# A new written order for a fused attention and two-MLP kernel, with the turns of the two array halves planned in it

## Chip, cores and metric

One core of one Trainium2 chip. The metric is the device time of one execution in microseconds (us); the kernel before takes 1275.89 us (median of 3 runs, 1275.63 to 1276.41). The work is done by TensorE (PE, with its weight loads shown apart as PEld), VectorE (DVE), ScalarE (ACT), GpSimd (POOL), and SyncE (SP), which starts the transfers.

## What is computed

The reference, cut to what matters. First a softmax-weighted sum over 7 neighbouring positions, per head; then two MLPs, the second with a rational function in the middle:

```python
w = exp(weight_gen - max); w = w / (sum(w) + 1e-9)          # [2, 4096, 8 heads, 7]
out[b, s, h, g] = sum_k w[b, s, h, k] * x_pad[b, s + k, h, g] # 8 heads x 24 = 192 columns
x = out.reshape(8192, 192)
h = x @ moe_w_in;  g = h * sigmoid(h);  x = g @ moe_w_out     # 192 -> 2048 -> 192
h = x @ moe2_w_in
P = a0 + a1*h + a2*h^2 + a3*h^3
Q = 1 + |b0|*|h| + |b1|*h^2
return (P / (Q + 1e-6)) @ moe2_w_out
```

## The kernel before

**Tiles.** The 8192 tokens are done in 16 batches of 512. In each batch both MLPs run over 8 units of 256 of the 2048 middle columns. Values are split in a high and a low part (`xh` and `xl`, `g1h` and `g1l`, `g2h` and `g2l`), and each product is the sum of three or so partial products. Weights are split alike (`wa`, `wb` for the first product of an MLP, `wo` for the second).

**The two halves of the array.** Nearly every matmul uses 64 of the 128 rows of TensorE's array: 9728 matmuls of 64 rows by 512 columns, half of them on the upper 64 rows (half 0), half on the lower (half 1). A matmul of half 0 and one of half 1 run side by side. A *turn* below is the time in which a half does one such matmul. A transpose of 64 columns counts as a quarter of a turn, as in the code (L808, L1015).

**Steps.** A step of TensorE is a small list of matmuls for each half. Its name gives the kind, the unit and the batch, so `K3.9` is step K of unit 3 in batch 9:

- `A`, `K` (first MLP) and `B`, `Q` (second): the first product of a unit, into a PSUM tile `h` of two banks. In `A` half 0 writes bank 0 and half 1 writes bank 1; in `K` it is the other way round.
- `C`, `E`, `I`, `F` (first MLP) and `D`, `P`, `J`, `R` (second): the second product, added into the tile `acc` of the batch. `C`, `I`, `D`, `J` need the high part, the others the low part; again each half writes one bank in two of them and the other bank in the other two.
- `T`, `TR` and `FT`, `FR`: transposes of the attention's result and of the batch's output, in the same two sides.

**A flip.** The two halves never write the same bank at once. Where a step changes which half writes which bank of a tile (K after A, Q after B, a change of side in an `acc`), `Lanes.take` puts a no-operation of SyncE between (L388): it waits for the last matmul of the old side in both halves, and the first matmul of the new side in each half waits for it. Such a change is called a flip here. Matmuls of other tiles may stand between the two sides and keep the array at work meanwhile.

**The other engines.** First MLP: ACT does `S` (silu) and `H` (high part), DVE `L` (low part). Second MLP: ACT `U`, `V`, `N`, `G`, DVE `u`, `w`, `Y`, `g`; then `h` (high part, L451, L453 or L455 on ACT, POOL or DVE) and `l` (low part, L987 on DVE or POOL). Attention products and sums (`M`, `m`, `p`, `r`, `a`) go to DVE or POOL. SP issues all transfers and also holds the flips' waits, in its own order.

**What sets the order.** The string `ORDER` is a list of 3956 steps, written out. Each entry may name an engine (`@1`), a buffer (`:c`), or a table load (`^`). `Plan.run` walks it. A step of TensorE is handed to `Lanes.add`, which puts its matmuls into the queues of the two halves; `Lanes.take` then writes them out one at a time into TensorE's single instruction stream. Which half comes next is decided by two clocks: that half whose clock is behind. A `|` before an entry pushes a clock on, so that one half falls behind the other on purpose:

```python
self.now = max(self.now, self.clock[r])
self.clock[r] = self.now + turns
```

Of the kernel before, what the change touches and what calls it, by code (L numbers as in the profile page):

```python
# [25 lines left out]
D = 192  # L26
# [23 lines left out]
    q0O341 A6.0:A s3m r3.1@1 q1B0a1 E5.0 C1.0 C3.0 a0.1@1:a r2.1@1 H4.0:v q0O3h a1.1 q1O0l0:q L4.0:p q1B0a0 K6.0  # L50
    q1O1l1:c q0O3x |F5.0 S6.0 a3.1@1 |||E4.0 q1B040:B H6.0:n F0.0 q1B041 F3.0 q1A0a0 q1O1l0:o a2.1@1 L6.0:m A7.0:D
    q1O0l1:s q1B0h0 m1.2:b q1A1l0:h F4.0 AW.3 I5.0 q1A040:A q1B0h1 K7.0 q1B0x0 M0.2:t C0.0 q1A0a1 q1B0x1 E6.0 M3.2:w
    S7.0 C6.0 q1A041 q1A0h@1 |T.1:B H7.0:i C4.0 m0.2:l TR.1 q1O0a0 s3d@1 C5.0 C7.0 XH0.1:p L7.0:j q1A1l1:a q1O2l1:e
    q1O2l0:x q1O0a1 q1O040:D |||||E7.0 q1A0x M1.2:q ||I4.0 F6.0 q1O041 I7.0 XL0.1:y q1O0h m2.2:v F7.0 q1O1a1 I6.0
    q1O0x q1O1a0 q1O140:A q1O141 ||||A2.1:D ||K2.1 M2.2:r m3.2@1:k q1A1a0 q1O1h p3.2@1 q1A1a1 EC.0@1:n q1A140:B
    q1O1x EM.0 S2.1 p2.2@1 X.3 q1A141 q1O3l0:c H2.1:s p0.2 q1O3l1:o q1A1h L2.1:v r0.2@1 A1.1:A K1.1 q1O2a0 p1.2@1 cr
    A0.1:D EA.0 S1.1 q1A1x XH1.0:h a0.2:n K0.1 r3.2@1 H1.1:m XL1.0:i A3.1:B S0.1 L1.1:t B0.0:C r1.2@1 a1.2 H0.1:k
    a3.2 q1O240:A K3.1 q1O2a1 r2.2@1 L0.1:l Q0.0 S3.1 m2.3:a q1O241 B5.0:D V0.0:x q1O2h@1 a2.2 H3.1:w m0.3:j q1O2x
    Q5.0 U0.0:r L3.1:b B3.0:A M0.3:u V5.0:g u0.0 F0.1:B Q3.0 p0.3@1 U5.0:q w0.0 F2.1 V3.0:e F1.1 I0.1 Y5.0 I1.1
    q1O3a0 F3.1 U3.0:j u5.0 B2.0:C u3.0 C1.1 ^^N5.0 E1.1 Y0.0 w3.0 Q2.0 G5.0 w5.0 E0.1 E3.1 q1O3a1 E2.1 U2.0:m  # L60
    B1.0:A N0.0 C2.1 q1O340:D q1O341 C0.1 g5.0 q1O3h Q1.0 V2.0:k q1O3x I2.1 h5.0:v u2.0 M2.3:g |A5.1:D V1.0:s U1.0:l
    w2.0 K5.1 r0.3@1 G0.0 u1.0 l5.0@1:b A4.1:C w1.0 C3.1 ^S5.1 K4.1 p2.3 g0.0 h0.0@2:t A7.1:A H5.1:c S4.1 I3.1
    l0.0@1:x H4.1:q K7.1 L5.1:f C5.1 S7.1 L4.1:o |A6.1:D H7.1:a Y1.0 r2.3@1 E4.1 K6.1 F4.1 S6.1 L7.1:p B4.0:C M3.3:y
    H6.1:r B6.0:A m3.3:o L6.1:w C6.1 E5.1 ^^N1.0 Y2.0 E7.1 Q4.0 G1.0 Y3.0 R0.0:D I6.1 F5.1 N2.0 g1.0 G2.0 R5.0
    h1.0@2:s D0.0 N3.0 g2.0 I5.1 s3e P0.0 l1.0:f F7.1 h2.0@1:k P5.0 M1.3@1:p Q6.0 U4.0:b l2.0@1:l s3t R1.0 G3.0 J1.0
    C4.1 V6.0:x E6.1 g3.0 s3n@1 D5.0 U6.0:r D1.0 F6.1 h3.0@1:c u6.0 I4.1 J0.0 Y6.0 V4.0:w s3s C7.1 l3.0@1:t P2.0
# [28 lines left out]
    N6.2 J1.2 FE.1@1 R5.2 M2.6:m A0.4:B G6.2 FA.1 EA.3 O.1 A1.4:A g6.2 XH1.3:a D3.2 G7.2 XL1.3:i h6.2:w P5.2 K0.4
    g7.2 B0.3:C ^S0.4 l6.2:r D6.2 H0.4:x m2.6@1:j Q0.3 h7.2@1:b L0.4:t p2.6@1 P6.2 K1.4 U0.3:d l7.2:j A2.4:B V0.3:l
    D4.2 M3.6:s S1.4 u0.3 |K2.4 H1.4:f s4d@1 w0.3 J4.2 S2.4 R7.2 L1.4:c R2.2 r0.6@1 H2.4:y B2.3:C Y0.3 B1.3:A L2.4:g
    ^^N0.3 Q2.3 M1.6@1:e E1.4:B V2.3:u R6.2 p3.6 C0.4 U2.3:k E0.4 Y2.3 Q1.3 G0.3 u2.3 w2.3 F1.4 I0.4 U1.3:v m1.6:c
# [179 lines left out]
class Plan:  # L278
# [25 lines left out]
    def run(self, engines, preload, lanes):  # L304
# [19 lines left out]
        for entry in ORDER.split():  # L324
            head, _, slot = entry.partition(":")
# [16 lines left out]
            else:  # L342
# [781 lines left out]
```

## Time and profile before

| | us |
|---|---|
| median of 3 runs | 1275.89 |
| the profiled execution, its own time | 1275.2 |
| span in its trace | 1273.4 |
| outside the span (launch and end) | 1.8 |
| PE busy | 1223.8 (96%) |
| DVE busy | 1096.0 (86%) |
| ACT busy | 1047.5 (82%) |
| POOL busy | 470.0 (37%) |

PE's busy time counts a matmul from its start to its modelled end, and two run side by side, so 96% busy is not 96% of what the array can do: the distance between the starts of two matmuls of the same half tells more. The granted clock of TensorE is at its full level (2.4 GHz) nearly all the time, with mean 0.991 over the span.

### The profile page before, as it was taken

Reading aid. Unit: us, or ns where it says so; the run is one execution under the profiler, and the core shown is the slowest. Engines: PE = TensorE matmul, PEld = TensorE weight load, DVE = VectorE, ACT = ScalarE, POOL = GpSimd, SP = SyncE. Lnnn points to the kernel's source line nnn. Section 1 sums busy time; section 2 is a strip of 40 time slices with the busy share of each in tenths; the row PEclk is TensorE's granted clock in tenths of the full one; section 3 lists DMA queues with packets and bytes.
Section 4 is the critical chain, followed back from the end, with each engine's and each line's share of the span. In section 5 each row is a group of like instructions: output and inputs, shape, how many; then the busy total and the mean of one; then the engine's idle time right before and its main releaser. Section 6 shows DMA issues by size and latency. Waiting matters only on the chain.

```text
span 1273.4 us, 24930 instructions
## 1 busy us (share of the span) xinstructions
PE 1223.8 (96%) x10332; PEld 1013.4 (80%) x10332; DVE 1096.0 (86%) x1037; ACT 1047.5 (82%) x1023; POOL 470.0 (37%) x311
## 2 busy tenths in 40 slices
PE   4889999999999999999999999999999999999997
PEld 4667777999888777789888787787777888898776
DVE  7889978999888879788989888878787989988897
ACT  3769788888988877698988788878888798899985
POOL 5565554344443422324232531440521513322322
PEclk8989999999999999999999999999999999999999
DMA  7650101010101010101002010010000001000000
GB/s 208 194 171 1 62 1 47 10 44 28 43 26 39 14 40 1 31 10 32 22 5 68 1 56 1 21 40 1 22 32 1 22 13 45 1 22 2 10 14 25
DMA packets 17753, 45.42 MB, mean 36 GB/s; under 512 B 2412, under 2 KB 9194, under 8 KB 17640
## 3 DMA queue, kind: packets, MB, share of 16 engines
q1 hardware_dynamic: 17640, 43.83, 11.2%
q8 instruction: 81, 1.33, 0.4%
q14 instruction: 32, 0.26, 0.1%
HBM read 31.73 MB, written 7.90 MB: 31 GB/s over the span
## 4 chain that ended last, share of the span: by engine, by line
PE 75%; ACT 8%; DVE 6%; issue 2%; SPq 1%; DMA 0%; POOL 0%; DVEq 0%; ACTq 0%
PE acc L795 38%; PE h L795 35%; DVE t L960 1%; ACT t L947 1%; ACT y L971 1%; ACT y L951 1%; DVE t L957 1%; ACT y L974 1%; PE to L1015 1%; PE tp L808 1%; ACT h L902 1%; ACT g1h L906 1%; DVE g1l L910 1%; SPq L928 1%; DVE t L977 1%
## 5 line engine op out<-in xcount | busy, mean ns | idle before, releaser
L795 PE MATMUL h<-xh,wa 64*128 64x512 f32 x2048 | 508.6, 401 | 13.2 <-DVE t L960 2.9
L795 PEld LDWEIGHTS h<-xh,wa 64*128 64x128 f32 x2048 | 303.1, 185 | 79.3 <-SPq L388 39.6
L795 PE MATMUL h<-xl,wa 64*128 64x512 f32 x1024 | 337.7, 390 | 0.1
L795 PE MATMUL h<-xh,wb 64*128 64x512 f32 x1024 | 336.2, 390 | 0.0
L795 PE MATMUL acc<-g1h,wo 64*128 64x512 f32 x1536 | 329.8, 397 | 4.9 <-DVE wo L623 1.8
L795 PE MATMUL acc<-g2h,wo 64*128 64x512 f32 x1536 | 311.3, 393 | 2.4 <-SPq L388 0.6
L795 PEld LDWEIGHTS acc<-g1h,wo 64*128 64x128 f32 x1536 | 224.3, 185 | 36.7 <-SPq L388 13.5
L987 POOL TENSOR_TENSOR g2l<-t,g2h 128x1024 fp32r<-128x1024 f32 x65 | 170.5, 2626 | 212.0 <-DVE g2h L455 98.0
L795 PEld LDWEIGHTS acc<-g2h,wo 64*128 64x128 f32 x1536 | 216.9, 184 | 31.0 <-SPq L388 11.4
L795 PE MATMUL acc<-g1l,wo 64*128 64x512 f32 x1024 | 239.9, 397 | 1.6 <-DVE g1l L910 0.7
L795 PE MATMUL acc<-g2l,wo 64*128 64x512 f32 x1024 | 236.4, 394 | 1.0 <-DVE t L960 0.3
L910 DVE TENSOR_TENSOR g1l<-h,g1h 128x1024 fp32r<-128x1024 f32 x128 | 155.6, 1220 | 62.6 <-ACT g1h L906 50.7
L957 DVE TENSOR_TENSOR t<-t,h 128x1024 f32<-128x1024 f32 x128 | 155.6, 1216 | 37.8 <-ACT y L951 19.9
L902 ACT ACTIVATE h<-h 128x1024 f32<-128x1024 f32 x128 | 129.3, 1011 | 70.8 <-PE h L795 65.2
L795 PEld LDWEIGHTS h<-xl,wa 64*128 64x128 f32 x1024 | 173.6, 185 | 14.7 <-DVE xl L829 0.8
L795 PEld LDWEIGHTS h<-xh,wb 64*128 64x128 f32 x1024 | 172.8, 185 | 14.1
L966 DVE SCALAR_TENSOR_TENSOR y<-y,b_sb 128x1024 f32<-128x1024 f32 x128 | 168.8, 1325 | 11.0 <-ACT y L951 10.8
L977 DVE SCALAR_TENSOR_TENSOR t<-t,a_sb,y 128x1024 f32<-128x1024 f32 x128 | 166.7, 1312 | 12.8 <-ACT y L974 11.5
L947 ACT ACTIVATE t<-h,a_sb 128x1024 f32<-128x1024 f32 x128 | 153.6, 1202 | 24.7 <-PE h L795 23.0
L795 PE MATMUL h<-xl,wb 64*128 64x512 f32 x512 | 169.3, 389 | 0.0
L960 DVE SCALAR_TENSOR_TENSOR t<-t,a_sb,h 128x1024 f32<-128x1024 f32 x128 | 163.5, 1279 | 6.5 <-ACT y L951 3.3
L728 POOL TENSOR_TENSOR pr<-xw,aw 128x768 f32<-128x768 f32 (+1 forms) x74 | 109.6, 1491 | 158.0 <-PE acc L795 82.0
(81 smaller groups left out, 1847.7 us busy)
## 6 DMA issues: line engine op xcount, KB each, us to landing
xw<-in_x_dram SPq DMA_DIRECT2D x14, 960.0 KB, 4.9
raw<-in_moe_w_out_dram SPq DMA_DIRECT2D x16, 383.5 KB, 5.1
out_dram<-of SPq DMA_DIRECT2D x15, 384.0 KB, 2.3
e<-e SPq DMA_DIRECT2D x32, 128.0 KB, 2.3
raw<-in_moe_w_in_dram SPq DMA_DIRECT2D x16, 255.9 KB, 6.6
raw<-in_moe_w_in_dram SPq DMA_DIRECT2D x4, 511.8 KB, 4.7
aw<-wsm SPq DMA_DIRECT2D x14, 112.0 KB, 2.4
sm<-in_weight_gen_dram SPq DMA_DIRECT2D x3, 448.0 KB, 3.4
```

The costliest lines, as they stand in the source:

```text
L728: e.tensor_tensor(out=p.rearrange("p k (h g) -> p k h g", g=G), in0=st[xw][:, j + k0:j + k0 + n, :].rearrange("p k (h g) -> p k h g", g=G) ...
L795: return pe.matmul(out=out, lhsT=w, rhs=x, start=start, stop=stop)
L808: return lambda: pe.transpose(out=st[tp][:, a, j * P + r * DL:j * P + (r + 1) * DL], in_=columns(a, j, r), identity=ident[HALF[r], HALF[r]],)
L902: act.activation(out=st[hb], in_=st[hb], func=AF.Silu)
L906: act.activation(out=t, in_=st[hb], func=AF.Copy)
L910: dve.tensor_tensor(out=t, in0=st[hb], in1=st[gh].bitcast(F32), op=ALU.subtract)
L947: act.activation(out=q, in_=st[hb], func=AF.Identity, scale=a_sb[:, 3:4], bias=a_sb[:, 2:3])
L957: dve.tensor_tensor(out=st[t], in0=st[t], in1=flat(), op=ALU.mult)
L960: dve.scalar_tensor_tensor(out=st[t], in0=st[t], scalar=a_sb[:, 1:2], in1=flat(), op0=ALU.add, op1=ALU.mult)
L966: dve.scalar_tensor_tensor(out=st[y], in0=st[y], scalar=b_sb[:, 0:1], in1=st[y], op0=ALU.add, op1=ALU.mult)
L977: dve.scalar_tensor_tensor(out=st[t], in0=st[t], scalar=a_sb[:, 0:1], in1=st[y], op0=ALU.add, op1=ALU.mult)
L987: e.tensor_tensor(out=q, in0=st[t], in1=st[gh].bitcast(F32), op=ALU.subtract)
```

## The change

Three things change together.

1. `ORDER` is another list of the same 3956 steps: other places, other buffers, and for some steps another engine.
2. The `|` marks are gone. 784 entries carry `>n` or `<n` instead: in this step half 1 stands n turns behind (`>`) or ahead of (`<`) half 0. An entry without a mark has both halves level.
3. `Lanes.add` gives each matmul a planned time when its step is added, and the writing-out goes by these times, rather than by clocks that move as matmuls are written out. `take` and `drain` only compare the times at the heads of the two queues. Flips are made as before.

```diff
+import re
 ORDER = """
-    r1.1@1 |||E3.0 H5.0:g q0O2x A4.0:B q1A0l1:u X.2 q0O3a0 p3.1@1 L5.0:k E1.0 K4.0 q0O3a1 q0O340:D r0.1@1 F1.0 S4.0
+    A6.0:A C3.0 K6.0<2 E3.0<2 p3.1@1 M1.1@1:w A7.0:D<1 H4.0:h S6.0 H6.0:j C4.0<1 L4.0:i q1O1l0:g K7.0<3 L6.0:q
...
-            name = entry.strip("^|").partition(":")[0].partition("@")[0]
+            name = re.split("[:@<>]", entry.lstrip("^"))[0]
...
+            entry, way, lag = re.match("([^<>]*)([<>]?)(.*)", entry).groups()
+            lag = int(lag or 0) * (-1 if way == "<" else 1)
...
-                    lanes.add(name, fn(engines[engine]), bars)
+                    lanes.add(name, fn(engines[engine]), lag)
...
-    def add(self, name, group, bars):
+    def add(self, name, group, lag):
         tile_key, side, turns, rows = group
+        self.clock[1] = max(self.clock[1], self.clock[0] + lag)
+        self.clock[0] = max(self.clock[0], self.clock[1] - lag)
         for r in range(2):
             for emit in rows[r]:
-                self.queue[r].append((name, tile_key, side, turns, emit))
+                self.queue[r].append((self.clock[r], name, tile_key, side, emit))
+                self.clock[r] += turns
         self.left[name] = sum(map(len, rows))
-        if bars:
-            r = self.clock[1] < self.clock[0]
-            self.clock[r] = min(self.clock[r] + bars, self.clock[1 - r])
         while all(self.queue):
-            self.take(self.clock[1] < self.clock[0])
+            self.take(self.queue[1][0][0] < self.queue[0][0][0])
...
-        self.now = max(self.now, self.clock[r])
-        self.clock[r] = self.now + turns
...
-            r = int(self.clock[1] < self.clock[0])
-            self.take(r if self.queue[r] else 1 - r)
+            self.take(bool(self.queue[1]) and (not self.queue[0] or self.queue[1][0][0] < self.queue[0][0][0]))
```

Two places on TensorE show what moves. A row is an instruction; `x2` is two alike in a row; a row that waits for `SP_sequencer` is the first matmul behind a flip.

**Unit 3 of batch 9, first MLP (A3.9, then K3.9).** Rows of `h` belong to A3.9 or K3.9, rows of `acc_7869` to step R of the batch at work in the second MLP. Before:

```order
L795 MATMUL h<-xh_8071,wb_75 128x512
L795 MATMUL acc_7869<-g2l,wo_78 128x512 [waits SP_sequencer_49]
L795 MATMUL h<-xl_8090,wa_71 128x512
L795 MATMUL acc_7869<-g2l,wo_78 128x512
L795 MATMUL h<-xl_8090,wb_75 128x512
L795 MATMUL h<-xh_8071,wa_71 128x512 [waits SP_sequencer_49]
L795 MATMUL acc_7869<-g2l,wo_78 128x512
L795 MATMUL h<-xh_8071,wa_72 128x512
```

and in the change:

```order
L809 MATMUL h<-xl_8097,wa_71 128x512 x2
L809 MATMUL h<-xl_8097,wb_75 128x512 x2
L809 MATMUL acc_7855<-g2h,wo_78 128x512 [waits Pool_49]
L809 MATMUL acc_7855<-g2h,wo_78 128x512 x4
L809 MATMUL h<-xh_8067,wa_71 128x512 [waits SP_sequencer_49]
L809 MATMUL acc_7855<-g2h,wo_78 128x512
L809 MATMUL h<-xh_8067,wa_72 128x512
```

Before, the last matmul of A3.9 stands right ahead of the first of K3.9. Now five matmuls of the second MLP's `acc` stand between them.

**Unit 1 of batch 6, first MLP (A1.6, then K1.6).** Before:

```order
L795 MATMUL h<-xl_5234,wa_71 128x512
L795 MATMUL h<-xl_5234,wb_75 128x512
L795 MATMUL h<-xh_5188,wa_71 128x512 [waits SP_sequencer_49]
L795 MATMUL h<-xh_5188,wa_72 128x512
L795 MATMUL acc_5252<-g2l,wo_78 128x512
```

and in the change:

```order
L809 MATMUL h<-xl_5159,wb_75 128x512 x2
L809 MATMUL h<-xh_5157,wa_71 128x512 [waits DVE_49]
...
L809 MATMUL h<-xh_5157,wa_72 128x512 x2
L809 MATMUL h<-xh_5157,wb_75 128x512 x2
L809 MATMUL h<-xl_5159,wa_71 128x512 x2
L809 MATMUL h<-xl_5159,wb_75 128x512 x2
L809 MATMUL h<-xh_5157,wa_71 128x512 [waits SP_sequencer_49]
```

Before, the last two matmuls of A1.6, both of half 1, are followed at once by K1.6. Now the whole of A0.6, the unit next to it, stands between.

## Rows read from the trace of the kernel before

**Rows 1.** The page: engines, and the chain that ended last by engine.

```profile
span 1273.4 us, 24930 instructions
...
PE 1223.8 (96%) x10332; PEld 1013.4 (80%) x10332; DVE 1096.0 (86%) x1037; ACT 1047.5 (82%) x1023; POOL 470.0 (37%) x311
...
PE 75%; ACT 8%; DVE 6%; issue 2%; SPq 1%; DMA 0%; POOL 0%; DVEq 0%; ACTq 0%
```

**Rows 2.** Windows of 50 us: their bounds, length, each engine's busy time, clock, DMA.

```profile
0.00:50.00 50.00, 30.66 (x207) 25.75 (x207) 41.57 (x55) 26.65 (x35) 25.25 (x28) 0.86 0.80 221
50.00:100.00 50.00, 45.11 (x317) 33.60 (x318) 40.07 (x52) 32.48 (x41) 34.09 (x29) 0.93 0.43 144
250.00:300.00 50.00, 50.00 (x439) 47.30 (x437) 48.99 (x47) 45.12 (x43) 22.40 (x14) 1.00 0.10 30
450.00:500.00 50.00, 47.89 (x382) 37.99 (x380) 41.27 (x37) 41.76 (x40) 10.37 (x5) 1.00 0.06 21
```

**Rows 3.** PE in order of time round the flip of K3.9: start, length, operation.

```profile
709.01 0.39 PE L795 MATMUL h<-xl,wa 64*128 64x512 f32 x1
...
709.23 0.39 PE L795 MATMUL h<-xl,wb 64*128 64x512 f32 x1
709.71 0.50 PE L795 MATMUL h<-xh,wa 64*128 64x512 f32 x1
...
710.05 0.39 PE L795 MATMUL h<-xh,wa 64*128 64x512 f32 x1
```

**Rows 4.** PE in order of time round the flip of Q3.5, batch 5.

```profile
491.26 0.39 PE L795 MATMUL h<-xl,wb 64*128 64x512 f32 x1
491.29 0.61 PE L795 MATMUL acc<-g1h,wo 64*128 64x512 f32 x3
491.78 0.49 PE L795 MATMUL h<-xh,wa 64*128 64x512 f32 x1
...
492.11 0.39 PE L795 MATMUL h<-xh,wa 64*128 64x512 f32 x2
```

**Rows 5.** PE in order of time round the flip of F3.7, batch 7.

```profile
574.21 0.39 PE L795 MATMUL h<-xl,wa 64*128 64x512 f32 x1
...
574.43 0.39 PE L795 MATMUL acc<-g1l,wo 64*128 64x512 f32 x1
...
574.66 0.53 PE L795 MATMUL acc<-g1l,wo 64*128 64x512 f32 x2
```

**Rows 6.** Weight loads that wait for SP: us in total, times, longest.

```profile
PEld h L795 <- SPq L388: 39.6, 86, 1.6
PEld acc L795 <- SPq L388: 32.6, 73, 1.4
```

**Rows 7.** Groups of instructions that change their engine or count.

```profile
L987 POOL TENSOR_TENSOR g2l<-t,g2h 128x1024 fp32r<-128x1024 f32 x65 | 170.5, 2626 | 212.0 <-DVE g2h L455 98.0 <-ACT g2h L451 56.7 <-DVE t L977 16.4
...
L987 DVE TENSOR_TENSOR g2l<-t,g2h 128x1024 fp32r<-128x1024 f32 x63 | 76.8, 1231 | 4.3 <-PE acc L795 2.0 <-POOL g2h L453 1.4 <-PE h L795 0.3
...
L451 ACT ACTIVATE g2h<-t 128x1024 fp32r<-128x1024 f32 x54 | 56.6, 1056 | 9.2 <-DVE t L977 4.8 <-PE acc L795 2.4 <-DVE ao L748 1.2
...
L453 POOL TENSOR_SCALAR g2h<-t 128x1024 fp32r<-128x1024 f32 x45 | 54.5, 1216 | 295.7 <-DVE t L977 114.1 <-DVE t L957 61.4 <-PE h L795 49.2
```

**Rows 8.** DVE's longest wait: us in total, times, longest.

```profile
DVE g1l L910 <- ACT g1h L906: 50.7, 48, 4.2
```

**Rows 9.** Matmuls that wait for SP: us in total, times, longest.

```profile
PE h L795 <- SPq L388: 2.4, 3, 1.2
PE acc L795 <- SPq L388: 2.3, 7, 0.9
```

**Rows 10.** Step Y on DVE: shortest, median and longest of 128.

```profile
L966 DVE SCALAR_TENSOR_TENSOR y<-y,b_sb x128: 1270/1277/2572, 105.5 to 1255.9; 128x1024 f32<-128x1024 f32 x128
```

**Rows 11.** One slow Y on DVE, and POOL at that time.

```profile
986.45 2.37 DVE L966 SCALAR_TENSOR_TENSOR y<-y,b_sb 128x1024 f32<-128x1024 f32 x1
...
985.32 5.77 POOL L987 TENSOR_TENSOR g2l<-t,g2h 128x1024 fp32r<-128x1024 f32 x2 [10.08 <-PE acc L795]
```

More of the change, by code (lines that the diff above doesn't have):

```diff
@@ L50 @@
[L50 to L54, printed above, removed]
@@ L95 @@
[L95 to L98, printed above, removed]
-    J7.2 V1.3:x F0.4 r3.6@1 X.7 B3.3:C N2.3 u1.3 p1.6@1 D7.2 s4e w1.3 P7.2 G2.3 Q3.3 r2.6@1 A3.4:A U3.3:j C2.4 Y1.3
@@ new lines @@
+    w6.10 V4.10:x U4.10:q A6.11:C h1.10:l l1.10:e F4.11 B7.10:B E5.11 u4.10 w4.10 Q7.10 l0.10@1:c p0.13 F5.11
+    V7.10:m h3.10:d l3.10@1:y I5.11 K6.11>2 M1.13:v A7.11:D>2 C5.11>2 U7.10:o u7.10 w7.10 S6.11 H6.11:s K7.11
+    r0.13@1 L6.11:k I6.11 J0.10:B>2 R1.10>4 S7.11 H7.11:h ^^N5.10 L7.11:p R0.10>4 Y6.10 C6.11>4 E6.11>2 N6.10 G6.10
+    P2.10>2 Y7.10 Y4.10 P3.10>2 N4.10 G4.10 P1.10>2 E7.11>2 P0.10>2 T.12:C>2 D3.10>2 F6.11 D2.10 g6.10 TR.12<2
+    I7.11<2 FT.9:D R3.10 R2.10 F7.11 J2.10 C7.11>2 FR.9 D0.10 g4.10 XH0.12:y G5.10 XL0.12:s A1.12:C<2 EC.11@1:i
@@ new lines @@
+    C1.12:C>4 C0.12>2 V1.11:n U1.11:w u0.11 w0.11 Y1.11 A3.12:A G3.11 F0.12 P6.10 D6.10 Y0.11 K3.12<2 E2.12<2
+    R6.10<2 N1.11 u1.11 w1.11 G1.11 E1.12<2 B5.11:D<2 I1.12<2 Q5.11 g1.11 g3.11 Y2.11 E0.12 N0.11 ^S3.12 H3.12:b
+    D5.10 L3.12:n U5.11:o V5.11:a m3.13:q h3.11:x I2.12<2 F3.12 I0.12 u5.11 w5.11 A4.12:A>2 ^^N2.11 G2.11 FC.10:i
+    p3.13 r3.13 E3.12>2 C3.12>2 A5.12:D g2.11 K4.12 K5.12 F2.12 B6.11:B I3.12 G0.11 ^S5.12 H5.12:n S4.12 H4.12:m
+    F1.12>2 Q6.11>2 g0.11 Y5.11 a3.13@1 m2.13:b L5.12:q C2.12>2 A7.12:D I4.12 U6.11:p V6.11:l L4.12:d K7.12>2
@@ new lines @@
+    A6.12:A>2 E4.12>2 C4.12>2 K6.12 h2.11@1:j S7.12 H7.12:f u6.11 w6.11 M2.13:e S6.12 p2.13@1 h0.11:c l0.11@1:k
+    H6.12:m C5.12 C7.12<2 Y6.11 r2.13 ^^N6.11 G6.11 B4.11:B<4 L7.12:y F4.12<4 I5.12<4 J2.11:D<2 F7.12 Q4.11 l2.11:b
+    L6.12:s P0.11 F6.12 a2.13@1 l3.11:n R0.11 T.13:A I6.12 g6.11 h1.11@2:e l1.11:v V4.11:t N5.11 Y4.11 TR.13>2
+    D3.11>2 G5.11 U4.11:k E7.12 P2.11 g5.11 P1.11 E6.12 P3.11 XH0.13:w XL0.13:d u4.11 E5.12 C6.12 J0.11<2 F5.12
+    I7.12 h6.11:m N4.11 h5.11@1:l G4.11 w4.11 l6.11@1:h g4.11 h4.11@2:q FT.10:A>2 D0.11>2 FR.10 D6.11 D1.11<2
@@ new lines @@
+    p2.14@1 K1.13<2 S1.13 R7.11<2 J6.11<2 FC.11:q H1.13:h L3.13:p M3.14@1:m L1.13:x A2.13:A B3.12:B m0.14@1:i Y0.12
+    FT.11:D K2.13 S2.13 FR.11 FE.11 FA.11 C0.13:C Q3.12<2 H2.13:k p0.14 L2.13:n I1.13<2 A5.13:D U3.12:s E0.13
+    r0.14@1 a0.14:e E3.13 r2.14@1 O.11 B1.12:A V3.12:i ^^N0.12 G0.12 I0.13 F3.13>2 Q1.12>2 V1.12:y C1.13>2 u3.12
+    w3.12 E2.13 E1.13 p3.14 Y3.12 B5.12:B Y1.12 I3.13 F0.13>2 U1.12:p u1.12 w1.12 Q5.12>2 N3.12 G3.12 U5.12:h
+    C3.13>2 g0.12 h2.12@2:q A4.13:A V5.12:f u5.12 w5.12 C2.13 r3.14 K4.13<2 ^S4.13 H4.13:o F2.13<2 a2.14@1 g3.12
@@ new lines @@
+    I3.14<2 L4.14:u M1.15:d g0.13 p1.15@1 Q5.13 E3.14 m2.15:x E2.14 A7.14:A A5.14:B U5.13:v V5.13:n F2.14 K5.14
+    S5.14 K7.14 I4.14 S7.14 H5.14:i u5.13 w5.13 Y5.13 r3.15 p2.15 H7.14:l r2.15@1 a2.15 h2.13:x L5.14:p A6.14:D>2
+    L7.14:w C4.14>2 K6.14 F4.14 FT.12:B F5.14 S6.14 H6.14:y FR.12 B7.13:A L6.14:g FE.12@1 FA.12 h1.13:e r1.15@1
+    a1.15 E4.14 E5.14 Q7.13 ^^G4.13 a3.15@1 g4.13 V7.13:s U7.13:m B6.13:D J2.13:B C6.14>2 E6.14 Q6.13 E7.14 C5.14
+    Y7.13 N5.13 G5.13 N3.13 u7.13 h4.13:d l4.13@1:u N7.13 V6.13:p J1.13<2 w7.13 T.15:A F7.14 F6.14 D4.13 G7.13
@@ new lines @@
+    h3.14@2:f A4.15:A>2 C0.15>2 K4.15 Q4.14 C1.15 L5.15:c A7.15:B<2 l3.14:t I5.15<2 S4.15 H4.15:x V4.14:e K7.15
+    g1.14 L4.15:i U4.14:b F5.15 A6.15:A S7.15 H7.15:q u4.14 E5.15 w4.14 K6.15 E4.15 E3.15 h1.14@1:p S6.15 E2.15
+    C4.15 C7.15<2 B6.14:C<4 h0.14:c l0.14@1:j I1.15<4 F4.15<2 I7.15<2 L7.15:g Y4.14 ^^N5.14 G5.14 H6.15:o I6.15
+    g5.14 Q6.14>2 C6.15>2 L6.15:r E6.15 C5.15 E7.15<2 P2.14:B<2 h5.14:w N4.14 G4.14 V6.14:h F7.15<1 F6.15 I4.15
+    g4.14 B7.14:A>2 Y6.14 U6.14:m u6.14 w6.14 FT.13:C>2 N6.14 EC.15:y h4.14@1:g l5.14:u D2.14>2 EM.15 FR.13 FE.13
@@ L267 @@
+    D3.15 P3.15<2 l6.15:b P5.15 g4.15 Y7.15 u7.15 h4.15@1:f l4.15@1:s N7.15 G7.15 w7.15 g7.15 h7.15@2:w l7.15:p
+    D6.15 P6.15<1 R6.15 J5.15 FT.14:C>2 R5.15>2 J4.15>2 J6.15>4 R4.15 O.13 D4.15 P4.15<2 D7.15<1 P7.15 FR.14 R7.15
+    J7.15 FE.14@1 FA.14 O.14 FC.15:v FT.15:D FR.15 FE0.15 FA0.15 FE1.15@1 O0.15 FA1.15 O1.15
 """
@@ L324, in run @@
         for entry in ORDER.split():
+            entry, way, lag = re.match("([^<>]*)([<>]?)(.*)", entry).groups()
+            lag = int(lag or 0) * (-1 if way == "<" else 1)
             head, _, slot = entry.partition(":")
-            table, bars, head = head.count("^"), head.count("|"), head.lstrip("^|")
+            table, head = head.count("^"), head.lstrip("^")
             name, _, e = head.partition("@")
@@ L364, in __init__ @@
         self.tc, self.sp = tc, sp
-        self.queue, self.clock, self.now, self.left, self.side = ([], []), [0, 0], 0, {}, {}
+        self.queue, self.clock, self.left, self.side = ([], []), [0, 0], {}, {}
         self.after = mybir.DependencyInfo(mybir.DependencyClass.Sync, mybir.DependencyReason.DATA)
-    def add(self, name, group, bars):
+    def add(self, name, group, lag):
         tile_key, side, turns, rows = group
+        self.clock[1] = max(self.clock[1], self.clock[0] + lag)
+        self.clock[0] = max(self.clock[0], self.clock[1] - lag)
         for r in range(2):
             for emit in rows[r]:
-                self.queue[r].append((name, tile_key, side, turns, emit))
+                self.queue[r].append((self.clock[r], name, tile_key, side, emit))
+                self.clock[r] += turns
         self.left[name] = sum(map(len, rows))
-        if bars:
-            r = self.clock[1] < self.clock[0]
-            self.clock[r] = min(self.clock[r] + bars, self.clock[1 - r])
         while all(self.queue):
-            self.take(self.clock[1] < self.clock[0])
+            self.take(self.queue[1][0][0] < self.queue[0][0][0])
     def take(self, r):
-        name, tile_key, side, turns, emit = self.queue[r][0]
+        _, name, tile_key, side, emit = self.queue[r][0]
         was = self.side.get(tile_key)
```

423 lines of the change are left out of this document (207 added, 216 removed).

## The prediction

> **What bounds the kernel now.** I read the page first: the chain that ended last lies 75% on PE, while DVE is busy for 86% of the span and ACT for 82% [rows 1]. So TensorE is to be looked at, but its 96% busy says little, because two matmuls run side by side and each counts until its modelled end.
>
> The windows tell more. From 250 to 300 us 439 matmuls ran in 50 us, that is 2 x 50 / 439 = 0.228 us for a turn of a half; from 450 to 500 us only 382 ran at the same full clock, 0.262 us a turn [rows 2]. There are 38 such matmuls to a unit of each MLP, 9728 / 2 = 4864 turns; at 0.23 us they would need 1119 us of the span of 1273.4 us. Some 150 us are therefore transposes, start, end and stalls of the array, and a stretch such as 250 to 300 us shows that stalls need not be.
>
> What differs between such stretches is seen at the flips, in order of time. At K3.9 the last matmul of the old side started at 709.23 us and the first of the new side at 709.71, where a free half would have gone on after 0.23: 0.25 us lost. The next of that half came at 710.05, 0.34 instead of 0.23 later: 0.11 more [rows 3]. A flip with nothing between costs about 0.37 us. At Q3.5 one turn lies between: the old side ends with the start at 491.26, the new side starts at 491.78 and goes on at 492.11. That is 0.06 more than two turns and then 0.10 more than one, 0.16 us lost [rows 4]. At F3.7 two turns lie between, and the starts follow one another at 0.22 and 0.23 us: nothing is lost [rows 5]. So from the last start of the old side to the first of the new some 0.5 us pass at the least, and other turns can fill them. In the view of waits, weight loads waited for SP, which holds the flips, 86 + 73 = 159 times and 39.6 + 32.6 = 72.2 us in all [rows 6].
>
> **The change, term by term.** I walked both orders through their own rules, counting a matmul as one turn and a transpose as a quarter, in the order of the stream. This gives counts, no time. From the first transposes of batch 1 on, turns between the two sides of a flip:
>
> | | none | one | two | more | all |
> |---|---|---|---|---|---|
> | before | 130 | 61 | 122 | 340 | 653 |
> | change | 17 | 47 | 206 | 399 | 669 |
>
> The flips in the first batch are left out, since the array waits for data there anyway. In the window from 250 to 300 us no flip has fewer than two turns between, from 450 to 500 eleven have: 7 with none, 4 with one, at these prices 3.2 us of the 6.5 that the window lacks (57 matmuls by 0.114).
>
> *Flips.* 113 fewer with none by 0.37 is 41.8 us, 14 fewer with one by 0.16 is 2.2 us: **-44.0 us**, all on PE's path. The bounds: nothing, if other waits fill the same time; at most 127 x 72.2 / 159 = 57.7 us, if each is worth the mean wait of a weight load. I take the prices at single flips, since they measure starts of matmuls, the thing that counts. The 16 extra flips have two turns or more between and cost nothing by [rows 5]; what hides them is the other tile's turns.
>
> The Trainium skill, "TensorE: Matmul & The Clock Gate", Part 3, says that the engine pulls weight loads ahead of matmuls in flight where the row groups differ. By that rule a weight load that waits might cost no matmul anything, and the gain would be next to nothing. The trace speaks against it here: in [rows 3] the matmuls themselves start late.
>
> *Turns out of step.* Where the stream gives one half two matmuls in a row, the other half can idle. By the same walk the stream is 4960.75 turns long before and 4952.5 after: 8.25 by 0.23 is **-1.9 us**. Between 0 and 2, since a half that idles may be waiting anyway.
>
> *Engines.* Step `l` moves 11 times from DVE to POOL, `h` 11 times from ACT to POOL. DVE loses 11 x 1.231 = 13.5 us, ACT 11 x 1.056 = 11.6, POOL gains 11 x (2.626 + 1.216) = 42.3 [rows 7]. None lies on the path as long as PE leads: DVE had 1273.4 - 1096.0 = 177.4 us idle, POOL 803. The attention's adds move a little both ways, and two of ACT's 81 table loads go; I put these at nothing, covered by the same idle time. The longer `l` on POOL delays only the steps P and R, which stand a median of 177 turns behind their Q now (164 before).
>
> *Data waits that come up.* A faster array has its data ready less early. From K to the first use of its low part the median is 43 turns now and 32 before, so the order gives more room than the shorter turns take. DVE kept up at 48.99 of 50 us while the array lost nothing [rows 2], and will be at about 1082.5 / 1235 = 88%. Still, the stretch from 450 to 500 us lacks as much again as its flips explain, and such waits can take part of what a flip gives back. I estimate one sixth of 44: **+7 us**, between 0 and 22 (half).
>
> *Start and end.* Until the first transposes of batch 1 the change has 85 DVE instructions instead of 79, but 146 turns done instead of 131, 15 x 0.23 = 3.4 us more work by that point. 317 matmuls between 50 and 100 us and the clock of 0.86 and 0.93 in the first two windows [rows 2] show a stage bound by data. I put it at **0**, between -6 and +6 us. At the end, 54 turns instead of 45 lie behind the last Q, to cover its chain through ACT and DVE: a microsecond or so, within that bound.
>
> *SP's queue.* SP holds the flips in order with its transfers, so a store that waits for its data delays flips behind it. The first flip behind a store of outputs now stands 23 turns or more after the transposes that the store needs in 13 of 15 batches, before in 2. No cost, at most a small gain.
>
> Sum, against the profiled execution of 1275.2 us: 1275.2 - 44.0 - 1.9 + 7 + 0 = 1236.3. The median of the runs is 0.7 above it, hence **1237 us**.
>
> **The rivals.**
>
> *DVE sets the pace.* Its idle time now is mostly waits for ACT, the longest 50.7 us for `g1h` [rows 8]. If its 177.4 us idle stay whatever PE does, the span is 1082.5 + 177.4 = 1259.9 and the time, with 1.8 us outside the span, 1262. For it: DVE's waits follow chains between ACT and DVE. Against it: it was 98% busy for 50 us in [rows 2]. Chance 0.10.
>
> *The flips are hidden anyway.* The matmuls that waited for SP by the page's count of idle time are only 2.4 + 2.3 = 4.7 us [rows 9], and if that is all they cost, the time stays at about 1275.9 - 4.7 - 1.9 = 1269, or at 1275 if other waits fill even that. Against it are the late starts; the count takes a matmul as busy until its modelled end, 0.39 us or more after its start, and so hides a gap. Chance 0.06. (The rule of the Trainium skill on weight loads, in "TensorE: Matmul & The Clock Gate", Part 3, would lead to this case.)
>
> *Slower: DVE slows beside POOL.* Step Y takes 1.277 us in the median and up to 2.572 [rows 10]; one of 2.37 us lies whole beside two `l` on POOL [rows 11]. More of `l` on POOL, placed beside Y and g (256 instructions on DVE), would make DVE the bound and longer. With its idle time kept (1262), it is slower from 256 x 0.064 us on, that is when Y and g take 0.064 us more in the mean; at 0.15 us more the time is 1262 + 38 = 1300. Against it: the median of Y lies at its shortest, 1.277 against 1.270 us, so few of them meet POOL now. Chance 0.04.
> The Trainium skill, "GPSIMD Engine Reference", section 1, says the same of the cause: POOL shares its SBUF interfaces with VectorE, and an instruction of VectorE with two SBUF inputs contends with it. By that rule every Y beside POOL would slow; the trace agrees for the one shown.
>
> **How the numbers follow.** The forecast has 0.80. Its lower end is 50 us won at the flips (half way to the higher price), nothing given back and 4 won at the start: 1275.9 - 50 - 1.9 - 4 = 1220. Its upper end is half of 44 given back and 6 lost at the start: 1275.9 - 22 - 1.9 + 6 = 1258. The range takes in the first rival's 1262 as well: **1220 to 1263**. The other two rivals, and what lies beyond these ends, are left out, 2 in 10 at most. About 0.2%, 2.5 us, is what a measurement can tell from no change. Faster: forecast and first rival, and most of the second, 0.93; within 0.2%: 0.03; slower: 0.04.
>
> **What would show it.** In the new profile weight loads should wait for SP some 60 times rather than 159, for about 25 us; windows of 50 us after the first 100 us should hold 430 or more matmuls nearly throughout; DVE should be busy for 87 to 89% of a span near 1235 us. It is wrong if those waits fall and windows still hold 400, with PE waiting for DVE or ACT instead; or if matmuls start 0.3 us or more apart at flips with two turns between.

## The result, and the profile after

The change takes 1209.88 us (median of 4 runs, 1208.21 to 1211.25) where the kernel before takes 1276.15 beside it (1275.63 to 1277.14): a ratio of 0.9479 with an interval of 0.9463 to 0.9496, 66.3 us or 5.2% less. The prediction said 1237 and a range of 1220 to 1263, so the time lies 10 us below the range. Its direction and its main mechanism, flips that find cover, hold; the gain is 1.7 times the 38.9 us that it gave.

The page of the change, engines and chain, as in [rows 1]:

```profile
span 1206.4 us, 24906 instructions
...
PE 1171.9 (97%) x10332; PEld 1038.9 (86%) x10332; DVE 1082.1 (90%) x1023; ACT 1035.7 (86%) x1011; POOL 508.0 (42%) x335
...
PE 78%; DVE 5%; ACT 4%; issue 1%; POOL 1%; SPq 0%; DMA 0%; DVEq 0%; ACTq 0%; POOLq 0%
```

The span is 67.0 us shorter than before. PE does the same 10332 matmuls; DVE and ACT each have 12 to 14 us less to do and wait less: DVE's idle time goes from 177.4 us to 1206.4 - 1082.1 = 124.3.

Windows of the change, columns as in [rows 2]:

```profile
0.00:50.00 50.00, 36.35 (x282) 32.22 (x284) 42.59 (x67) 30.01 (x39) 18.46 (x24) 0.97 0.82 213
50.00:100.00 50.00, 45.20 (x348) 34.88 (x344) 44.52 (x55) 42.83 (x51) 31.15 (x27) 0.97 0.49 152
250.00:300.00 50.00, 50.00 (x458) 46.29 (x456) 45.46 (x42) 45.00 (x46) 22.56 (x15) 1.00 0.13 39
...
350.00:400.00 50.00, 47.70 (x412) 41.44 (x410) 46.51 (x42) 45.42 (x42) 25.91 (x15) 1.00 0.19 63
450.00:500.00 50.00, 50.00 (x462) 44.41 (x460) 44.15 (x39) 44.18 (x44) 23.17 (x14) 1.00 0.09 27
...
1150.00:1200.00 50.00, 48.47 (x400) 39.03 (x396) 46.04 (x39) 40.96 (x41) 19.30 (x8) 1.00 0.03 9
```

The stretch from 450 to 500 us, which held 382 matmuls [rows 2], holds 462. The first 50 us hold 282 instead of 207. From 150 us on, the thinnest window before the last one holds 412.

Weight loads that wait for SP, as in [rows 6]:

```profile
PEld h L809 <- SPq L405: 7.4, 14, 1.2
...
PEld acc L809 <- SPq L405: 6.1, 15, 0.8
```

29 waits and 13.5 us stand where 159 and 72.2 stood. The flip that the prediction read first, K3.9, shows why. PE in order of time there, to be held against [rows 3]:

```profile
662.99 0.42 PE L809 MATMUL h<-xl,wb 64*128 64x512 f32 x2
663.21 0.85 PE L809 MATMUL acc<-g2h,wo 64*128 64x512 f32 x5
663.71 0.39 PE L809 MATMUL h<-xh,wa 64*128 64x512 f32 x1
663.91 0.39 PE L809 MATMUL acc<-g2h,wo 64*128 64x512 f32 x1
663.95 0.58 PE L809 MATMUL h<-xh,wa 64*128 64x512 f32 x2
664.18 0.39 PE L809 MATMUL h<-xh,wb 64*128 64x512 f32 x1
```

Five matmuls of `acc` run between the two sides, and the first three starts of the half that opens the new side are 663.71, 663.95 and 664.18: a turn apart, nothing lost.

**Where the time came from.** I went through the starts of all matmuls in both traces. In the steady stretches a matmul starts 0.227 us after the one two places before it, in both kernels (median). What a start is late beyond that, halved because two halves share it, I call its loss. Losses of the six starts round a flip are put to that flip, and flips are sorted by the number of matmuls that stand in the instruction stream between the last one of the old side and the first one that waits. From the first transposes of batch 1 on:

| matmuls between | none | 1 to 3 | 4 or 5 | 6 and more | lost at flips | lost elsewhere |
|---|---|---|---|---|---|---|
| before: flips | 97 | 72 | 113 | 371 | | |
| us lost (mean) | 47.0 (0.48) | 14.2 (0.20) | 6.8 (0.06) | 8.5 (0.02) | 76.5 | 40.9 |
| change: flips | 13 | 16 | 202 | 438 | | |
| us lost (mean) | 6.6 (0.51) | 2.9 (0.18) | 4.9 (0.02) | 7.5 (0.02) | 21.9 | 36.0 |

The flips won 54.6 us and the other waits 4.9. The start won some 8 more: the first transposes of batch 1 begin at 68.0 us instead of 72.9, with 28 matmuls more in the stream ahead of them, 14 turns or 3.2 us. Together that is 67.6 us, where the time fell by 66.3; the other 1.3 us were lost elsewhere or are the error of this count.

### The profile page after: what moved, and what is told of

Same layout as the page of the kernel before. It is cut to its first block, busy times and chain, and to the rows that moved or that the text cites. A ratio compares the mean times of both kernels' runs of the same rounds, so it can differ in the third digit from the quotient of the medians.

```text
span 1206.4 us, 24906 instructions
## 1 busy us (share of the span) xinstructions
PE 1171.9 (97%) x10332; PEld 1038.9 (86%) x10332; DVE 1082.1 (90%) x1023; ACT 1035.7 (86%) x1011; POOL 508.0 (42%) x335
## 4 chain that ended last, share of the span: by engine, by line
PE 78%; DVE 5%; ACT 4%; issue 1%; POOL 1%; SPq 0%; DMA 0%; DVEq 0%; ACTq 0%; POOLq 0%
PE acc L809 40%; PE h L809 37%; DVE y L980 1%; POOL g2l L1001 1%; DVE t L971 1%; DVE t L974 1%; PE to L1029 1%; ACT y L988 1%; PE tp L822 1%; DVE t L991 1%; ACT y L985 1%; ACT g2h L465 0%; ACT y L965 0%; ACT t L961 0%; ACT g1h L920 0%
## 5 line engine op out<-in xcount | busy, mean ns | idle before, releaser
L809 PE MATMUL h<-xh,wa 64*128 64x512 f32 x2048 | 437.9, 393 | 7.7 <-DVE t L974 4.1
L809 PEld LDWEIGHTS h<-xh,wa 64*128 64x128 f32 x2048 | 277.7, 184 | 44.6 <-SPq L405 7.4
L809 PE MATMUL h<-xh,wb 64*128 64x512 f32 x1024 | 296.9, 388 | 0.0
L809 PE MATMUL h<-xl,wa 64*128 64x512 f32 x1024 | 296.6, 388 | 0.1
L809 PE MATMUL acc<-g1h,wo 64*128 64x512 f32 x1536 | 287.6, 392 | 0.2
L809 PE MATMUL acc<-g2l,wo 64*128 64x512 f32 x1024 | 201.4, 391 | 0.1
L809 PE MATMUL acc<-g1l,wo 64*128 64x512 f32 x1024 | 197.0, 394 | 0.2
L924 DVE TENSOR_TENSOR g1l<-h,g1h 128x1024 fp32r<-128x1024 f32 x128 | 155.8, 1220 | 41.3 <-ACT g1h L920 35.9
L467 POOL TENSOR_SCALAR g2h<-t 128x1024 fp32r<-128x1024 f32 x56 | 68.3, 1223 | 266.2 <-DVE t L991 108.4
L742 POOL TENSOR_TENSOR pr<-xw,aw 128x576 f32<-128x576 f32 (+1 forms) x73 | 114.4, 1580 | 140.1 <-PE acc L809 83.3
L965 ACT ACTIVATE y<-h,b_sb 128x1024 f32<-128x1024 f32 x128 | 141.8, 1111 | 25.9 <-PE h L809 20.0
```

The lines of the kernel that those rows point to most:

```text
L467: pool.tensor_scalar(out=out, in0=in_, scalar1=1.0, scalar2=0.0, op0=ALU.mult, op1=ALU.add)
L742: e.tensor_tensor(out=p.rearrange("p k (h g) -> p k h g", g=G), in0=st[xw][:, j + k0:j + k0 + n, :].rearrange("p k (h g) -> p k h g", g=G) ...
L809: return pe.matmul(out=out, lhsT=w, rhs=x, start=start, stop=stop)
L924: dve.tensor_tensor(out=t, in0=st[hb], in1=st[gh].bitcast(F32), op=ALU.subtract)
L965: act.activation(out=q, in_=st[hb], func=AF.Abs, scale=b_sb[:, 1:2])
```

## The experiments

The change has three parts: the order (with its buffers and engines), the end of the pushes with planned times in their place, and the lags. My theory after the result was the prediction's, with a higher price for flips: what counts is how many turns stand between the sides. The rival was that the new rule for turns brings the gain by itself, whatever the order. The buffers, and the engines of other steps than those named below, were not tried apart from the order.

**The lags at zero.** All else is the change's.

```diff
-            lag = int(lag or 0) * (-1 if way == "<" else 1)
+            lag = 0
```

> The changed kernel with every lag set to 0 (both halves level in each step), nothing else. Counts by the same walk: flips with none/one/two/more turns between 13/37/34/585 (the change: 17/47/206/399), but the stream is 5299.5 turns long instead of 4952.5, since steps whose lists differ in length now leave one half two in a row (1024 such places instead of 114). Theory 'flips and turns' (a flip with none costs some 0.4 us, one with one turn 0.17, a turn of the stream 0.23): 347 x 0.23 = 80 us more, 3 us less at flips, so 1282 to 1292. Rival 'the order of the other engines brings the gain, TensorE's turns are covered': within 10 us of the change, 1205 to 1220.

1215.53 us, ratio 0.9527 (0.9513 to 0.9541): only 5.6 us are lost, so the theory in that form misses by far. The time lies where the rival, the order of the other engines, put it; the runs with the order of before and those with extra flips, below, speak against that rival. The theory walked the stream with the two halves held in step, which makes this stream 347 turns longer, 80 us. The array did not do that. In the stream, six matmuls of J7.6 (`acc<-g2h`; halves 0, 1, 0, 1, 1, 1) stand ahead of six of C1.8 (`acc<-g1h`; halves 0, 1, 0, 1, 0, 0). PE in order of time in this kernel:

```profile
602.92 0.73 PE L809 MATMUL acc<-g2h,wo 64*128 64x512 f32 x4
603.37 0.39 PE L809 MATMUL acc<-g1h,wo 64*128 64x512 f32 x1
603.49 0.39 PE L809 MATMUL acc<-g2h,wo 64*128 64x512 f32 x1
603.60 0.39 PE L809 MATMUL acc<-g1h,wo 64*128 64x512 f32 x1
603.72 0.39 PE L809 MATMUL acc<-g2h,wo 64*128 64x512 f32 x1
```

The first matmul of C1.8 starts at 603.37, ahead of the last two of J7.6 (603.49 and 603.72), which stand before it in the stream. A half whose next matmul stands behind some of the other half's starts it anyway. So three in a row of one half, which occur 512 times here, cost little, and a count of turns with the halves in step overstates both this cost and the number of flips with nothing between (130 by that walk, 97 in the stream).

The Trainium skill, "TensorE: Matmul & The Clock Gate", Part 3, has matmuls start strictly in program order. Between the two halves this trace shows otherwise, 0.12 us out of order, and the trace decides.

**The order alone, under the old clocks.** The kernel before with the change's `ORDER`; the lags are stripped from its entries, and no entry has a push.

> The changed kernel's order (without its lags) under the turn rule of before (two clocks, no pushes). Flips 30/143/94/402, stream 4937.75 turns. Theory 'flips and turns': 13 x 0.4 + 96 x 0.17 - 3 = 18 to 20 us above the change, 1225 to 1231. Rival 'the order alone brings the gain': as the change, 1205 to 1215. Rival 'the planned times bring the gain': near the kernel before, above 1260.

1216.29 us, 0.9531 (0.9517 to 0.9545): 59.9 of the 66.3 us, more than expected and close to what the rival 'the order alone brings the gain' said. 18 flips have nothing between, and flips lose 27.3 us.

**The new rule alone, with the order of before.** The change with the `ORDER` of before, pushes stripped, all lags zero.

> The order of before (without its pushes) under the turn rule of the change with all lags 0. Flips 14/33/49/557 instead of 130/61/122/340, stream 5296.75 turns instead of 4960.75. Theory 'flips and turns': 336 x 0.23 = 77 us more, 116 x 0.4 + 28 x 0.17 = 51 us less than the kernel before, so 1295 to 1305. Rival 'the planned times bring the gain by themselves': under 1240.

1221.70 us, 0.9575 (0.956 to 0.9589): 54.4 us won without any step moved. This is what the rival said; but the pushes are gone here as well, and the next run takes that part by itself. Weight loads that wait for SP:

```profile
PEld h L795 <- SPq L391: 9.1, 13, 1.8
...
PEld acc L795 <- SPq L391: 4.7, 8, 1.0
```

21 waits instead of 159, and 14 flips with nothing between. Planned times write the two open steps out evenly, one side of a tile among the matmuls of another, so almost every flip gets its cover from the rule.

**The pushes alone taken away.** The kernel before, old clocks and order, every `|` removed:

```diff
-    r1.1@1 |||E3.0 H5.0:g
+    r1.1@1 E3.0 H5.0:g
```

> The kernel before without its 82 pushes, nothing else. Flips 80/42/165/366 instead of 130/61/122/340, stream 4941.75 turns instead of 4960.75. Theory 'flips and turns': 50 x 0.4 + 19 x 0.17 + 19 x 0.23 = 27 us less, so 1245 to 1253. Rival 'the other engines' order sets the time': within 5 us of the kernel before.

1237.89 us, 0.97 (0.9684 to 0.9716): 38.3 us, again more than expected, by an edit that moves no step. The pushes had been put there to set the halves apart; they left 97 flips bare, that is with nothing between, and without them 40 are. Flips lose 44.0 us instead of 76.5. Weight loads that wait for SP, to be held against [rows 6]:

```profile
PEld h L795 <- SPq L388: 23.4, 53, 2.0
PEld acc L795 <- SPq L388: 19.1, 45, 1.4
```

So the parts overlap. Without pushes: old clocks and old order 1237.9, new order 1216.3, new rule 1221.7, both 1215.5, and with the lags 1209.9. Either part alone removes most bare flips, and the second finds few left.

**More flips put in.** To measure the price itself, the change with an extra flip at the first matmul of each step E and P, and in a second kernel of E, P, F and R. It adds waits and moves nothing.

```diff
-        if was is None or was[0] != side:
+        again = name[0] in "EP" and name[1] != "E" and name not in self.again
+        if was is None or was[0] != side or again:
+            if again:
+                self.again.add(name)
```

> The changed kernel with an extra flip ahead of every step E and P (183 more after the first batch): a no-operation of SP waits for the matmuls before on that tile and the step waits for it, though no bank changes hands. Counted by matmuls in the stream between the old side's last and the wait, flips are 110 with none, 21 with 1 to 3, 211 with 4 or 5, 487 with more (the change: 13, 16, 202, 438). Theory 'a flip costs by what stands right ahead of it in the stream', at the losses measured so far (0.48, 0.20, 0.05, 0.02 us each): 49 us more, 1250 to 1268. Rival 'flips were a mark of a bad order, the array would have waited anyway': under 1225.

> As the run before, with an extra flip ahead of F and R too: 204, 25, 217, 539. Theory: 96 us more than the change, 1295 to 1315, twice the step of the run before. If data waits hide under the stalls, less than twice: 1280 to 1290. Rival: under 1235.

1254.94 us (0.9836, 0.9821 to 0.985) and 1309.03 us (1.0255, 1.0239 to 1.027): 45 and 99 us more than the change, as expected. In all, counting those that merely moved, there are 684 flips in the change, 849 and 1011 in these, so each one more costs 45 / 165 = 0.27 and 99 / 327 = 0.30 us, bare and covered ones together. 97 and 191 of them are bare (110 and 204 instead of 13), and at the 0.48 us of a bare flip that alone is 47 and 92 us. Weight loads that wait for SP, in the first:

```profile
PEld acc L813 <- SPq L409: 45.6, 93, 1.0
```

and in the second:

```profile
PEld acc L813 <- SPq L409: 87.0, 172, 1.3
...
PEld h L813 <- SPq L409: 7.1, 13, 1.9
```

The waits of weight loads grow by 39.0 and 80.7 us (all tiles together, from 14.2) and the time by 45 and 99, which rules out that flips are hidden anyway. A part is taken back: counted as in the table above, and to within some 1.5 us, flips lost 55 and 109 us more than in the change, while the other waits lost 27 and 22 us instead of 36.

**The engines at the start.** Twelve steps of the softmax and of the first batch's attention go back to the engine that they had before, in the change's order. Ten of them lie at the start; two (`s5d`, `s5n`) belong to a later softmax, near 590 us. The diff shows one line of the edit.

```diff
-    q0B040:B q0A0a0 q0A0l1:l m1.0@1:o q0O0l0:n M3.0@1:q m0.0@1:d p0.0 p1.0 r0.0
+    q0B040:B q0A0a0 q0A0l1:l m1.0:o q0O0l0:n M3.0:q m0.0@1:d p0.0 p1.0@1 r0.0
```

> The changed kernel with the engines of the softmax steps and of batch 0's attention steps as before (12 steps, most back from DVE to POOL); flips and stream unchanged. Theory 'the start is shorter because DVE works alone, without POOL beside it': the first product starts 3 us later than in the change (28.9 us) and the time is 2 to 4 us longer, 1212 to 1215. Rival 'the start is shorter because of the order of loads and weight steps': within 1 us of the change.

1218.56 us, 0.9546 (0.9531 to 0.956): 8.7 us slower than the change, more than twice what I expected. Only 4.3 us of it lie at the start: the first transposes of batch 1 begin at 72.3 us instead of 68.0. The first 30 us of the change, then of this kernel (columns as in [rows 2]):

```profile
0.00:30.00 30.00, 16.71 (x118) 15.95 (x120) 24.12 (x40) 13.19 (x18) 7.39 (x14) 0.94 0.89 217
```

```profile
0.00:30.00 30.00, 14.28 (x97) 13.87 (x98) 24.28 (x28) 11.25 (x15) 16.56 (x19) 0.95 0.85 211
```

DVE is busy for the same 24 us, but does 28 instructions instead of 40; POOL is busy for 16.56 us instead of 7.39. Two groups of DVE in that stretch (operation, shapes, count, busy, mean ns), in the change:

```profile
L742 DVE TENSOR_TENSOR pr<-xw,aw 128x576 f32<-128x576 f32 x4 | 3.0, 752 | 0.0
L752 DVE TENSOR_TENSOR pr<-pr 128x576 f32<-128x576 f32 x4 | 2.9, 752 | 0.0
```

and with the engines of before:

```profile
L742 DVE TENSOR_TENSOR pr<-xw,aw 128x576 f32<-128x576 f32 x3 | 4.1, 1352 | 0.0
...
L752 DVE TENSOR_TENSOR pr<-pr 128x576 f32<-128x576 f32 x3 | 3.4, 1159 | 0.0
```

The same instructions take 1352 and 1159 ns instead of 752 with attention work on POOL beside them. The work that POOL takes over is partly paid back by DVE. The granted clock of these 30 us is no part of the difference: 0.94 in the change, 0.95 here.

The Trainium skill, "GPSIMD Engine Reference", section 1, names the cause as the SBUF interfaces that POOL shares with VectorE; the two rows agree with it.

Most of the rest of the 8.7 us comes in the middle. The delay against the change, matmul by matmul, is 5.4 us at 593 us and 9.1 us at 605, where DVE now does the two steps of the later softmax and TensorE waits for DVE. In this kernel:

```profile
576.88 3.33 DVE L527 TENSOR_TENSOR sm<-sm 128x896 f32<-128x896 f32 x1
...
598.24 1.09 DVE L541 TENSOR_TENSOR sm<-sm 128x896 f32<-128x896 f32 x1
...
600.52 0.67 PE L809 MATMUL h<-xh,wa 64*128 64x512 f32 x1 [1.83 <-DVE g1l L924]
```

In the change POOL does these two, and no matmul waits for DVE there.

**The engines of h and l.** In the change's order, 135 steps `h` and `l` take the engine that the same step had before.

> The changed kernel with the engine of every h and l of the second MLP as before (135 steps change engine, 11 of each kind fewer on POOL in sum); flips and stream unchanged. Theory 'flips and start': within 4 us of the change, 1206 to 1214. Rival 'the shift of work to POOL gives part of the gain': 1217 or more.

1278.65 us, 1.0024 (1.0011 to 1.0037): the whole gain is gone, where I had expected next to nothing. The rival's number is met, but work moved to POOL cannot by itself be worth 69 us: in its own order the same choice of engines takes 1221.70 us (the new rule alone). Flips lose only 31.7 us here; the rest is in other waits, 95.5 us instead of 36.0. Matmuls that wait, in this kernel:

```profile
PE h L809 <- DVE t L974: 14.5, 12, 3.0
...
PE h L809 <- DVE g1l L924: 10.5, 11, 3.6
PE acc L809 <- POOL g2l L1001: 5.1, 7, 1.7
```

In the change the first of these is 4.1 us. So the engine of a step belongs to its place in the order: with another order, the old choice makes matmuls wait for DVE in places where they did not. This says nothing on the 11 more of `h` and `l` on POOL alone, which I did not try apart from the rest.

**Other lags.** A search over the entries of the change for lags that leave fewer flips with few matmuls between set 154 lags otherwise:

> The changed kernel's order with lags chosen anew, by a search that counts matmuls in the stream between the two sides of a flip and the distance at which the halves end a step, and nothing else. Flips with none/1 to 3/4 or 5/more between: 13/0/67/589 (the change: 13/16/202/438), the same counts as with all lags 0, but with the halves ending their steps closer together. Theory 'the stream counts': 16 flips fewer with 1 to 3 between are worth 16 x 0.18 = 3 us, the fewer with 4 or 5 another 1 to 2, so 1203 to 1208. Rival 'what is left after the flips is data waits, and lags move those too': within 3 us of the change or as with lags 0, 1208 to 1216.

1221.12 us, 0.9568 (0.9555 to 0.9581), 11 us slower than the change with its flips better by count (13, 0, 67 and 589 in the four classes, as with lags at zero). What its expectation says of the halves at the ends of steps is void, since that figure is the same for any lags. The flips with 6 and more between lost 18.4 us instead of 7.5. In its stream one half has four or more matmuls in a row 231 times, in the change 5 times; with lags at zero never, but three in a row 512 times.

The same search on the order of before found no lag to set, so that kernel is the one with the new rule alone, and its time a repeat:

> The order of before under the turn rule of the change, with lags chosen by the same search. Flips 14/0/73/566, as with lags 0 (1221.7 us), halves closer together at the ends of steps. Theory: what then parts it from the change is the start alone (8 to 13 us), so 1215 to 1222. Rival 'the order of steady batches is worth as much as the start': 1225 or more, or, if lags matter as much as in the change, below 1215.

1222.39 us, 0.9581 (0.9568 to 0.9594), 0.7 us from the first time.

A third search counted both, flips and such runs of one half, and set 37 lags otherwise; the change itself ran again beside it.

> The changed kernel with 37 lags chosen anew, for flips counted in the stream and, unlike the search before, against stretches in which the stream gives one half several turns in a row. Flips 13/0/203/453 (the change: 13/16/202/438), stretches of 3 or more turns of one half 36 (the change 22, the search before 289). Theory 'the stream counts, for flips and for how evenly the halves alternate': 16 x 0.18 = 3 us less than the change, 1205 to 1208. Rival 'the change's lags fit its data waits, and any other lags lose': 1211 or more.

> The changed kernel itself, unaltered, beside the run before on the same chip: 1208 to 1212 by either theory.

1211.71 us (1209.72 to 1212.24; 0.9496, 0.9483 to 0.9509) against 1209.48 (1209.24 to 1210.81; 0.9485, 0.9472 to 0.9498): no gain, as the rival said, and no lags that I found beat the change's. Lags are worth 5.6 us against none at all and can cost as much. That runs of four and more of one half cost time, and runs of three hardly any, fits these kernels; no run tells it apart from what else the lags move, so it stays open, and so does why the change's lags lose 6.1 us less away from flips than lags at zero (36.0 and 42.1 us).

## Why the prediction was right or wrong

The forecast missed by 27 us, and the range by 10, on three of its terms. Data waits were to come up by 7 us and fell by 4.9; a flip was priced too low; and the start, put at 0, won some 8 us. What it held of flips is the mechanism that the runs show.

**Flips: right in kind, too small.** 44.0 us were forecast and 54.6 came. The term that was mis-sized is the price. "113 fewer with none by 0.37" and "14 fewer with one by 0.16" were read at one flip each, [rows 3] and [rows 4]. Over all flips a bare one costs 0.48 and one with one to three between 0.20, and in the classes of the stream 84 fewer bare ones give 40.4 us, 56 fewer with one to three 11.3, and the others 2.9. The count was wrong as well, too high for bare flips (113 fewer forecast, 84 came) and far too low for the next class: it held the halves in step, which the lags at zero showed the array does not. The higher price that the prediction kept as a bound (57.7 us, by the mean wait of a weight load) was the nearer one.

**Turns out of step: priced by a mechanism that isn't there.** 8.25 turns at 0.23 made little here, so no harm came of it. The same price gave 80 us for lags at zero, which cost 5.6.

**Engines: the totals right, the zero for a reason that doesn't carry.** DVE's busy time was to fall by 13.5 us and fell by 13.9 (to 1082.1), though Y and `g` took 9 us more and other instructions as much less; ACT 11.6 and 11.8; POOL was to gain 42.3 and gained 38.0. Groups of the change against [rows 7] and [rows 10]:

```profile
L1001 POOL TENSOR_TENSOR g2l<-t,g2h 128x1024 fp32r<-128x1024 f32 x76 | 195.0, 2570 | 136.1 <-ACT g2h L465 36.6 <-PE h L809 32.9 <-DVE g2h L469 31.6
...
L980 DVE SCALAR_TENSOR_TENSOR y<-y,b_sb 128x1024 f32<-128x1024 f32 x128 | 175.9, 1381 | 5.6 <-ACT y L965 5.0
```

76 of `l` are on POOL, 11 more, as counted. But "nothing, covered by the same idle time" was judged by totals. With the engines of before in this order the time is 69 us longer, though DVE has only 1123.6 us to do in a span of 1275.6: cover is a matter of place, and sums over the span do not show it.

**Data waits that come up: wrong sign.** +7 us were put there, on the idea that a faster array finds its data less early. Other waits lost 36.0 us instead of 40.9. The idea itself shows where only flips are added: with 55 us more lost at flips the other waits lost some 9 us less, about the one sixth that was forecast. What failed is the level it started from, which was taken to stay and fell with the change. Why it fell is open. The order's greater room from K to the first use of its low part, which the prediction named and gave no price, is not shown to be the reason: counted the same way, other waits lost some 40 us with the change's order under the old clocks, 33 with the order of before without pushes, and 37 with the new rule on the order of before. DVE's longest wait [rows 8] fell too:

```profile
DVE g1l L924 <- ACT g1h L920: 35.9, 46, 2.6
```

**Start and end: 0 was too little.** The stage was read rightly as bound by data, but 6 more DVE instructions and 15 more turns were weighed without the price of DVE's instructions beside POOL. Some 8 us came, though the first matmul starts 2.4 us later (11.0 instead of 8.6). The engines account for 4.3 of the 4.9 us by which the first transposes of batch 1 come earlier; the rest is mostly the 14 turns that the order has done by then.

Flips, data waits and start come to 10.6 + 11.9 + 8.1 = 30.6 us. Less the 1.9 that turns out of step were to bring, and the 1.3 that went elsewhere, that is the 27 us by which the forecast missed. The low end missed because it took 50 us at the flips, 4 at the start and nothing won at the data waits.

**The rivals.** *DVE sets the pace* fell: its idle time did not stay at 177.4 us. *The flips are hidden anyway* fell by the extra flips. *DVE slows beside POOL* happened, too little and with room to spare: the mean of Y rose by 0.056 us (1.325 to 1.381) and that of `g` by 0.016 (1.312 to 1.328), 0.036 for the two, where it asked for 0.064 and for DVE's idle time to stay, which fell by 53 us. Every Y of over 1.3 us overlaps an operation of POOL (11 before, 21 in the change), but some that lie beside POOL from end to end take 1.27 to 1.32 us, so "every Y beside POOL would slow" does not hold here.

**What was to show it.** Waits of weight loads for SP: some 60 in 25 us were forecast, 29 in 13.5 us came. Windows of 430 matmuls or more nearly throughout: from 250 to 300 and 450 to 500 us yes, from 350 to 400 us 412. DVE at 87 to 89%: it is at 90% of a shorter span.

## What to carry to other kernels

Where two users of an engine hand over through a semaphore, count what stands between the two sides in the instruction stream, and take the price from all such hand-overs in the trace, not from one of each kind. Before a new order is searched for, try the rule that writes it out: here deleting the old pushes won 38 us, and planned times without any lag 54 (the pushes gone with them), with no step moved. An engine choice found with one order is part of that order, and is not to be carried over to another by totals.

## What the runs showed that was not expected

- The two halves of the array do not wait for each other's place in the stream: a matmul of one half started 0.12 us ahead of two of the other half that stand before it.
- The price of a flip falls off fast with what stands between: 0.48 us with nothing, 0.20 with one to three matmuls, 0.06 with four or five, 0.02 beyond, though the count alone doesn't settle it (four or five: 0.02 in the change; six and more: 0.02 in the change, 18.4 / 589 = 0.03 with other lags).
- Attention work on POOL made DVE's instructions of one shape take 1159 and 1352 ns in the mean instead of 752.
